# A convolution and token-mixing kernel: stretches of 64 rows in four quadrants of TensorE

## The chip, the core and the metric

The kernel runs on one core of a Trainium2 chip. The metric is the device time of one execution in microseconds (us). A profile of one execution is at hand; "span" is the time from its first to its last instruction. The engines are called by the profile's names: PE is TensorE's matmul, PEld its weight load, DVE is VectorE, ACT is ScalarE, POOL is GpSimd (it issues the loads of x here), SP issues the other transfers.

## What is computed

Eight batches of x, 4224 rows by 192 columns, go through a causal convolution along the rows: seven taps, one set of weights for each of 8 heads of 24 columns, with the weights put through a softmax. On its result y a token mixer follows:

```python
w = softmax(weight, axis=-1)                      # 8 heads x 7 taps
y[b, s, h, :] = sum_k w[h, k] * x_pad[b, s + k, h, :]   # 6 rows of zeros ahead
W_tok = scale * (y @ w_q) @ (y @ w_k).T           # 4224 x 4224 for each batch
out = relu(W_tok @ y) @ w_out
```

The kernel never makes the 4224 x 4224 matrix. It forms the Gram matrix y.T @ y (192 x 192) of a batch, multiplies it by w_k into mixing weights of 64 x 192, and applies these to y @ w_q. Matmuls are in bf16 with sums in f32.

## The kernel before

**Tiling of x and the convolution.** A batch is cut into 35 chunks of 122 rows (`CW`, `NCC`). For each chunk a window of 128 rows of x, six of them shared with the chunk before, lies across the 128 partitions: `XW[:, slot, chunk, :]`, cast from f32 to bf16 by the transfer itself. Five batches of x have a slot (`NX`). A matrix `BAND[:, h, :]` (128 x 128) holds the taps of head h along its diagonals. `gen_conv` multiplies it with the 24 columns of the head of all 18 or 17 chunks of a group at once, so with 432 or 408 moving columns (batch 0 has four smaller groups). It is done as one matmul over the whole array (line 356) or as two matmuls on the two column halves (lines 357 and 358); helper `halves` chooses by the mode of the operation. VectorE or ScalarE then copies the result to `Y` as bf16 (line 693).

**From y to the output.** `gen_transpose` turns the low 128 columns of each chunk (line 362 whole, lines 363 and 364 by column halves), eight chunks to a bank of the accumulation memory, and VectorE copies them to `YTL` (line 724). `gen_transpose_hi` turns the high 64 columns of two chunks side by side (line 754), copied to `YTH` (line 764). `gen_wq` projects both with w_q (lines 783 and 787) into `WQT`. `gen_gram` accumulates the Gram matrix, three matmuls a chunk (line 821). `gen_mix_weights` makes the mixing weights. `gen_mix` applies them (lines 914, 926 and 934), takes the ReLU into `RT` (lines 951 and 952), multiplies with w_out (lines 980 and 998), copies to `OUT` (line 1019) and stores.

**Shapes of the array.** An operation on TensorE has a mode: the whole array (128x128), two column halves (128x64) or two row halves (64x128). In the profile a matmul's shape stands as rows*columns: `128*64` or `122*64` is a column half, `64*128` a row half, `128*128` or `122*128` the whole.

**The order of the work.** All operations are generated in a simple order and numbered as they come. The string `PLAN`, written out by hand or by a program, then sets the order in which they are handed to the engines: `43S` is operation 43 on SP, `80P3` operation 80 on TensorE with bank 3, F in place of P means the whole array, A, D and G are ScalarE, VectorE and GpSimd. Each engine works through its operations in that order; waits between the engines come from the dependences (`Program.place`). Loads of a batch wait for the convolution of the batch that had the slot before.

**The start.** TensorE multiplies zeros (`run_up`, line 382, 512 columns each) while the taps are computed: four, then five of these, then two fills of the taps' bands (`spread`), then one more, and then the convolution of batch 0. The first load of x is the first thing that POOL issues, before it builds the identity matrix.

Of the kernel before, what the change touches and what calls it, by code (L numbers as in the profile page):

```python
# [13 lines left out]
PLAN = """  # L14
42G 0S 43S 1D 23A 2D 14G 9D 5D 6D 7D 4D 41G 45G 46G 47G 48G 62G 63G 64G 65G 16P3 10D 11D 12D 15D 20D 21D
17P2 19A 18P5 22D 24D 25D 26D 28A 27A 44A 49S 29D 31D 30D 32D 33D 34P4 37P1 40P7 38D 39D 3D 35A 78P0 36A
80P3 81D 82P1 83A 84P7 85D 79A 114P3 140P7 92P0 93A 66G 67G 115D 90F1 91A 88F6 89D 86F0 87A 98F4 99D 13D
94F6 95A 100F5 50S 101A 96F0 116F3 97A 117D 142P 141P 102F2 103D 108F5 109A 104F4 106F3 107D 8D 51S 118F0
119D 124P6 125D 105A 122F5 123D 120F4 121D 144P 126P2 127D 128P1 129D 143P 145P 146D 54A 52A 53A 130P6 131D
138P7 139A 132P3 159P1 160D 161A 56A 156F4 157A 158D 153F6 154A 155D 162F1 163A 164D 136P0 137D 134P5 135D  # L20
133A 55A 147F4 148A 181F7 182D 183F6 184D 207P4 174P0 175D 176D 168P2 59A 57A 58A 149P5 152A 151A 150A 165P6
209P 171P0 166A 167D 249P5 169D 170A 172A 173D 208P 235P6 252D 238A 61A 221P0 224A 185P1 186D 195P7 196D
191P5 192D 220P2 222A 60A 68G 189P6 190D 223D 287P0 187P7 211P 205P2 206D 188D 210P 193P5 194D 290P2 288A
289A 291D 292A 293P0 294A 295A 284P6 285D 286A 212P 199P5 200A 69G 299P2 300A 197P1 198A 213D 214P0 301D
234P6 215D 236D 237A 225P4 229P2 226P 227A 248P0 250A 251A 230P 231D 232D 263P6 266A 228D 233S 70G 71G 314P7
315D 203P4 204A 201P2 277P3 279A 72G 73G 74G 75G 76G 77G 110G 111G 112G 113G 177G 178G 179G 180G 308G 309G
239P0 243P5 276P4 278D 240P 241D 202A 242A 312F7 313D 244F 245D 246A 247S 216F4 218A 262P0 264D 217A 265A
219A 253P2 257P6 280P5 254P 255D 256A 258P 259A 281P 282D 283S 305P0 306A 352P4 296P2 297A 298A 302P5 303A
338P0 260D 261S 307D 418P1 419A 420A 355A 340P 311G 304D 320P3 321D 324P5 325D 351P6 353D 354A 316F1 317D
366F2 369A 424F3 425D 426A 430F6 431D 432A 310G 342P 322P2 326P1 327D 271P4 323D 267P6 318F3 319D 272F 273A  # L30
274D 268F 269D 270A 275S 427F1 428D 429A 380F3 383D 334P4 335A 336P5 337D 339P 421P6 422A 423D 415P1 416A
417D 330P4 331A 332P3 333A 365P6 367D 368A 360P1 356P4 361P 362D 363A 357P 407P6 409D 358D 359A 364S 328P3
329A 394P7 397A 374P1 370P5 375P 376A 377D 379P3 371P 372A 373D 378S 381A 441F7 433F1 434D 435A 436F5 437D
438A 442D 408P3 341P 343P 344D 447P6 448D 451P5 452D 439P2 440D 345P7 410A 382A 384P3 346A 393P0 395A 388P5
347F7 349A 348A 396D 350A 385F 386A 387D 389F 390A 391D 392S 445F0 446D 478P1 480A 481D 402P3 411P5 398P6
403P 404D 405A 412P 413A 414S 399F 548F0 549D 550D 400A 401A 406S 443F4 444D 493P5 560P2 561A 562A 496D
479P6 482A 453P0 449P7 542P1 543A 454D 465P4 450D 545P5 546A 547D 461P3 462A 459P1 460D 507P0 510A 468P
506P6 508D 509A 463P5 557P0 558A 559D 544D 455P3 456A 464A 469P 563P6 564A 565D 551P0 552A 553D 466P 457P5
458D 483P6 492P2 494A 495D 487P0 484F 485D 486A 568F5 569D 488F 489D 490A 491S 497P2 470P 535P7 537A 554F5
555D 556A 498F 499D 500A 566F7 567D 521F1 524A 501P5 520P2 522A 523A 534P0 536A 502P 503D 504D 505S 467P  # L40
576P1 577D 574F7 575D 675F2 676D 677D 471A 472F5 473A 538P4 515P0 511P6 570F5 571D 474F2 477A 476A 475A 539F
540D 541S 572F3 573D 516P 517A 518D 512P 513A 514A 519S 525P4 578P2 580P0 581D 526F 527A 528D 669F6 670A
648F3 651A 672F0 671A 678F4 590P6 591A 679A 579D 586P2 587A 680A 592P3 594P 582P7 583A 673D 674D 606P0 620P6
609D 529P1 605P4 607D 530P 531A 634P7 637D 532A 533S 608A 623D 595P 584P0 585A 588P2 597P 589A 614P4 633P6
635A 636D 610P0 615F 616A 617D 693F2 694D 611P 661P6 612A 613D 618S 619P4 621D 593P 662P7 622A 664A 596P
647P1 628P4 663A 624P6 649A 650A 598D 599F3 600D 629F 630A 631D 625F 626A 627D 632S 684F0 685A 686D 601F2
604A 603A 602A 695F4 696D 642P6 638P0 643F 644D 645A 690F2 691A 692D 681F4 682D 683A 639F 640D 641A 646S
687F6 688D 689A 656P2 652P4 665P1 657P 658D 659A 653P 666P 667D 668S 733P0 736A 747P7 750D 703P6 704D 705P3
706D 654A 655A 660S 707P2 708D 796P0 797A 798A 697P7 698D 802P5 803A 804D 805P3 761P0 764A 806D 799P1 800A
801A 699P5 700D 732P6 701P0 702D 807D 709P3 710D 734A 811P1 812D 813A 717P0 718D 715P6 716A 735A 822P5 823D  # L50
820P3 821D 713P1 714A 711P2 712A 737P6 746P4 748A 749D 741P0 738F 739A 740D 775F2 778A 742F 755P4 788P3
751P6 743A 744D 745S 756P 757A 758A 760P1 762A 763D 790D 752P 753A 719P0 721P 808P4 754A 759S 789P3 929P1
723P 809A 810D 817P6 818D 819D 938P4 939D 940A 791A 724P 722P 720P 725A 930D 931A 774P6 776D 777A 765P4
792P3 769P0 793P 794A 795S 766P 767A 768D 770P 726P2 771D 772A 773S 727A 814P6 815A 846P3 848P 728P5 730A
729A 731A 816D 828P7 829D 824P6 825D 834P2 926P0 835D 826P4 827D 923P5 924D 832P2 833D 830P7 831D 927A 928A
925A 932P0 933A 842P4 860P6 863D 847P 844P7 845D 874P5 877D 934A 843D 840P1 841A 836P0 837D 851P 783P6 779P1
859P4 861D 862A 784P 785A 786A 780P 781D 850P 888P0 891A 782D 787S 849P 852A 935P5 838P4 936A 937D 839A
853P2 854D 949P3 950D 868P0 873P6 864P4 875D 876A 902F2 905A 869F 870A 871D 865F 866A 867D 872S 947F3 948D
901P6 903A 915P2 917D 882P0 904A 878P4 883P 884A 885D 916P3 918A 879P 880D 881A 886S 887P6 889D 890A 855F2
858A 944F0 945D 946A 941F3 942A 943D 857A 856A 919P5 910P6 892P0 911P 912D 913A 896P3 920P 921A 922S 893P  # L60
897P 898D 951P2 952D 959P7 961P6 962D 957P5 958D 953P3 954D 960D 894A 895A 899A 900S 955P0 956D 973P4 987P1
990D 971P2 972A 1001P5 1004A 963P6 964A 967P7 968A 906P2 986P0 988D 989A 907P 1014P5 908D 909A 914S 1016A
1017D 978P 1015P7 1018A 976P 1000P0 1002D 1003A 991P2 995P5 992P 993D 994A 1029F7 1032A 996P 997A 998D 999S
1009P0 1005P2 1010P 1011A 1012A 1028P6 1006P 1007A 1008D 1013S 1042P5 1044D 1030A 1031D 977P 974P 975P 979D
1043P2 1045A 965P0 966D 1023P5 1019P2 980F4 981D 1024F 1025D 1026A 1020F 1021D 1022A 1027S 982F7 985A 983A
984A 1033P0 1046P6 1034P 1035D 1036A 1037P4 1047P 1048D 1049S 1050P2 1052A 1038P 1039A 1040D 1041S 969P7
1051P6 1054A 1081F0 1066F5 1069A 1053D 970D 1065P1 1067D 1068A 1055P3 1056P 1057D 1058A 1059S 1084A 1060P6
1070P1 1061P 1062D 1063A 1064S 1080P4 1082A 1083D 1071F 1072A 1073D 1074S 1096F0 1099A 1075P6 1095P3 1097D
1098A 1076P 1077D 1078A 1079S 1090P1 1091P 1092A 1093D 1094S 1110P0 1112D 1100P3 1085P6 1101P 1102D 1103A
1104S 1111P5 1086P 1087D 1113A 1114P4 1105P2 1115P 1116A 1117S 1106P 1088D 1089S 1107D 1108D 1109S  # L70
""".split()

COL2, ROW2, FULL = "128x64", "64x128", "128x128"


class Op:
# [4 lines left out]
    def __init__(self, engines, emit, ns, needs=(), after=(), banks=0, drains=None, vt=0.0, mode=COL2, tail=0.0, whole=False):  # L81
# [12 lines left out]
        self.mode = mode  # L94

        self.whole = whole
# [12 lines left out]

        self.size = 0  # L110
        Op.n += 1
        self.id = Op.n


class Planner:

    ENGINES = {"P": "PE", "F": "PE", "A": "ACT", "a": "ACT", "D": "DVE", "d": "DVE", "G": "POOL", "S": "SP"}
# [106 lines left out]
def bass_lightweight_conv__then__hypermixer_token_mlp_kernel(  # L224
# [427 lines left out]
    def gen_conv(b, gi):  # L652
# [6 lines left out]
        for hp in range(H // 2):  # L659
# [25 lines left out]
            def evac(e, op, t0, t1, hp=hp, mm=mm):  # L685
                o = mm.bank * 512
                if nb == 1:
                    t0, t1 = 0, 2
# [424 lines left out]
```

## Time and profile before

| what | value |
|---|---|
| three runs | 167.82, 168.00, 168.57 us; median 168.0 |
| span of the profiled execution | 167.4 us |
| TensorE busy | 155.4 us, 2843 matmuls |
| VectorE, ScalarE busy | 132.4 us, 118.5 us |
| copies of y (line 693) | ScalarE 33.8 us in 71, VectorE 31.6 us in 57 |
| copies of the transposed y (lines 724 and 764) | VectorE, 40 and 24 of them |
| queue of x loads | 35616 packets, 13.41 MB as written |
| queue of stores and other loads | 12528 packets, 26.71 MB |

The time of a run is taken outside the program, so it lies a little above the span of the profiled execution. A busy time of TensorE is not a measure of its work, since matmuls overlap and their ends are modelled; the steps from one start to the next are.

### The profile page before, as it was taken

The numbers are of one execution on the slowest core, as the hardware profiler recorded it, in microseconds if no ns is written. First come the engines' busy times: TensorE is split into PE (matmuls) and PEld (weight loads), VectorE is DVE, ScalarE is ACT, GpSimd is POOL, SyncE is SP. The second block draws the span as 40 slices with busy tenths as digits, with TensorE's granted clock in tenths as the row PEclk, the third lists the DMA queues.
The fourth block names the chain that finished last, engine by engine and source line by source line (L and its number), as shares of the span: only waits on it lengthen the run. The fifth ranks groups of instructions, "written<-read, shape, count | busy, mean of one in ns | idle before, by whom it ended". The sixth has DMA issues, their size and how long they took to land.

```text
span 167.4 us, 6574 instructions
## 1 busy us (share of the span) xinstructions
PE 155.4 (93%) x2843; PEld 117.7 (70%) x2851; DVE 132.4 (79%) x277; ACT 118.5 (71%) x288; POOL 30.2 (18%) x39
## 2 busy tenths in 40 slices
PE   7589999999999999999999999999999999999930
PEld 2277948887777677787776768779888767785620
DVE  5554889987979699888976789976798888878950
ACT  3426357879975978877597788985856895969920
POOL 7999553535400200000000000000000000000000
PEclk9957999999999999999999999999999999999997
DMA  1999999999999999999999999999330585487996
GB/s 41 205 190 185 205 191 193 192 194 191 265 326 272 269 267 317 290 289 192 285 292 289 254 284 315 319 230 367 125 112 4 221 341 215 193 306 279 377 366 235
DMA packets 48172, 40.52 MB, mean 242 GB/s; under 512 B 37136, under 2 KB 40976, under 8 KB 48144
## 3 DMA queue, kind: packets, MB, share of 16 engines
q0 software_dynamic: 35616, 13.41, 66.8%
q1 hardware_dynamic: 12528, 26.71, 44.4%
q8 instruction: 22, 0.36, 0.9%
q14 instruction: 6, 0.05, 0.1%
HBM read 27.56 MB, written 25.95 MB: 320 GB/s over the span
## 4 chain that ended last, share of the span: by engine, by line
PE 85%; ACT 5%; DMA 2%; DVE 2%; issue 2%; DVEq 0%
PE ps L821 15%; PE ps L980 12%; PE ps L998 9%; PE ps L357 7%; PE ps L356 6%; PE ps L783 5%; PE ps L914 5%; PE ps L362 5%; PE ps L754 5%; PE ps L787 4%; PE ps L363 4%; PE ps L934 3%; PE ps L358 3%; DMA wt_f<-in_weight_dram 2%; ACT rt L951 2%
## 5 line engine op out<-in xcount | busy, mean ns | idle before, releaser
L951 ACT ACTIVATE rt<-ps 128x512 bf16<-128x512 f32 (+1 forms) x70 | 37.7, 560 | 5.9 <-PE ps L914 3.7
L693 ACT CAST y<-ps 122x432 bf16<-122x432 f32 (+2 forms) x71 | 33.8, 519 | 11.2 <-PE ps L358 9.1
L1019 DVE COPY out_sb<-ps 128x384 f32<-128x384 f32 (+1 forms) x64 | 32.8, 540 | 6.1 <-PE ps L998 4.6
L1019 ACT COPY out_sb<-ps 128x384 f32<-128x384 f32 (+1 forms) x72 | 31.5, 479 | 8.8 <-PE ps L998 8.2
L693 DVE CAST y<-ps 122x408 bf16<-122x408 f32 (+2 forms) x57 | 31.6, 587 | 6.5 <-PE ps L358 3.1
L578 POOL DMA_DIRECT2D xw<-in_x_dram x34 | 29.8, 904 | 25.1 <-issue 16.9
L821 PEld LDWEIGHTS ps<-y 122*64 122x64 bf16 x840 | 29.4, 112 | 3.6 <-issue 0.9
L821 PE MATMUL ps<-y 122*64 122x192 bf16 (+2 forms) x840 | 31.9, 223 | 0.0
L952 DVE TENSOR_SCALAR rt<-ps 128x512 bf16<-128x512 f32 (+1 forms) x42 | 26.0, 628 | 6.3 <-PE ps L914 4.6
L724 DVE COPY ytl<-ps 128x976 bf16<-128x976 bf16 (+1 forms) x40 | 23.2, 588 | 4.0 <-PE ps L364 3.0
L998 PE MATMUL ps<-wol,rt 64*128 64x192 bf16 (+1 forms) x264 | 25.1, 248 | 0.7 <-PE ps L998 0.3
L980 PE MATMUL ps<-woh,rt 64*128 64x192 bf16 x264 | 22.9, 248 | 0.8 <-ACT rt L951 0.4
L357 PE MATMUL ps<-xw,band 128*64 128x432 bf16 (+2 forms) x82 | 19.6, 347 | 0.1
L358 PE MATMUL ps<-xw,band 128*64 128x432 bf16 (+2 forms) x82 | 19.6, 349 | 0.0
L998 PEld LDWEIGHTS ps<-wol,rt 64*128 64x128 bf16 (+1 forms) x264 | 15.9, 114 | 4.4 <-PE ps L980 1.0
L804 ACT CAST wqt<-ps 128x512 bf16<-128x512 f32 (+1 forms) x26 | 13.7, 547 | 6.6 <-PE ps L787 6.5
L980 PEld LDWEIGHTS ps<-woh,rt 64*128 64x128 bf16 x264 | 12.5, 113 | 7.9 <-issue 1.7
L980 PE MATMUL ps<-wol,rt 64*128 64x192 bf16 x175 | 15.4, 243 | 0.0
L783 PE MATMUL ps<-ytl,wql 128*64 128x512 bf16 (+1 forms) x72 | 14.7, 367 | 0.2
L787 PE MATMUL ps<-yth,wqh 128*64 128x512 bf16 (+1 forms) x72 | 14.9, 361 | 0.0
L914 PE MATMUL ps<-wqt,msb 64*128 64x512 bf16 (+1 forms) x72 | 13.8, 363 | 0.0
L356 PE MATMUL ps<-xw,band 128*128 128x408 bf16 (+3 forms) x62 | 12.9, 333 | 0.1
(118 smaller groups left out, 207.9 us busy)
## 6 DMA issues: line engine op xcount, KB each, us to landing
out_dram<-out_sb SPq DMA_DIRECT2D x28, 768.0 KB, 7.2
xw<-in_x_dram POOLq DMA_DIRECT2D x7, 816.0 KB, 36.5
xw<-in_x_dram POOLq DMA_DIRECT2D x7, 768.0 KB, 38.6
out_dram<-out_sb SPq DMA_DIRECT2D x8, 384.0 KB, 4.3
out_dram<-out_sb SPq DMA_DIRECT2D x8, 96.0 KB, 5.2
xw<-in_x_dram POOLq DMA_DIRECT2D x1, 432.0 KB, 7.8
xf<-in_x_dram SPq DMA_DIRECT2D x1, 384.0 KB, 4.7
xw<-in_x_dram POOLq DMA_DIRECT2D x1, 384.0 KB, 6.3
```

Source lines behind the costliest of these rows:

```text
L357: e.matmul(out[0:64], lhsT[:, 0:64], rhs, **k)
L358: return e.matmul(out[64:128], lhsT[:, 64:128], rhs, **k)
L578: lambda e, op, part=part: e.dma_start(*part),
L693: return e.copy(dst, src) if op.engine == "ACT" else e.tensor_copy(dst, src)
L724: lambda e, op: e.tensor_copy(YTL[:, b % NYT, t0:t1], bank(mm_l.bank).bitcast(BF16)[:, 0:cols]),
L783: last = e.matmul(ps[64 * i : 64 * i + DH, 0:n], WQL[:, :], YTL[:, b % NYT, starts[i] : starts[i] + n], start=True, stop=False)
L821: mm = e.matmul(bank(where.bank)[p : p + 64, o : o + z - r], Y[0:w, yb, c, r : r + 64], Y[0:w, yb, c, r:z], start=st, stop=end, skip_group ...
L951: return e.activation(dst, src(), AF.Relu)
L952: return e.tensor_scalar(dst, src(), 0.0, None, op0=ALU.max)
L980: last = e.matmul(bank(op.bank + a)[:, (i - q) * D : (i - q) * D + D], RT[p, slot, a if lo else 2, i:n:nt], WOL[p, :] if lo else WOH[p, :] ...
L998: last = e.matmul(bank(fh.bank + a)[:, (i - q) * D : (i - q) * D + D], RT[p, slot, a, i:n:nt], WOL[p, :], start=False, stop=True, skip_gro ...
L1019: return e.copy(dst, src) if op.engine == "ACT" else e.tensor_copy(dst, src)
```

## The change

Stretches have 58 rows instead of 122, from windows of 64 rows. There are 37 on the lower 64 partitions, for the first half of a batch, and 36 on the upper 64, for the second half. The first window of the batch begins with 16 rows of zeros. Four batches of x have a slot instead of five.

The convolution runs in 64x64 mode: two row halves (first and second half of the batch) by two column halves (even and odd stretches), so that each step of a head is four matmuls on the four quadrants, with 240 and then 216 columns. `Y` then holds two stretches in one column, 64 partitions each, so 37 columns (19 and 18) with 116 rows of the batch each.

```diff
-    CW = 128 - (KC - 1)
-    NCC = (S + CW - 1) // CW
+    CW = 64 - (KC - 1)
+    NCC = -(-S // (2 * CW))
...
-    NX, NY, NYT = 5, 3, 2
+    NX, NY, NYT = 4, 3, 2
...
-    run_2 = run_up(5, after=[turned])
+    run_2 = run_up(12, after=[turned])
...
-    run_3 = run_up(1, after=fills)
+    run_3 = run_up(3, after=[fill])
...
+                for i in range(hn):
+                    h = hn * hp + i
+                    for r in range(2):
+                        rows, n = slice(64 * r, 64 * r + 64), ns[r]
+                        for p in range(2):
+                            last = e.matmul(
+                                bank(op.bank + r)[64 * p : 64 * p + 64, i * n * GRP : (i + 1) * n * GRP],
+                                BAND[rows, h, :],
+                                XW[rows, slot, 2 * g[0] + p : 2 * (g[0] + n) : 2, GRP * h : GRP * h + GRP],
+                                start=True,
+                                stop=True,
+                            )
```

Each half of the batch has a bank of its own and its own copy to `Y`: 480, 480, 432 and 384 columns where before 432 and 408 stood. The loads of a group are one for each half of the batch, and the rows behind the zeros make a third in the first group.

The low transpositions run in 64x128 mode, the two stretches of a column of `Y` on the two row halves, into two banks; the high ones run in 64x64 mode, four at a time. The copies out of them take both banks at once and put the stretches back in order, in pieces of 58:

```diff
+    TG = [(0, 10), (10, NA)]
+
+    def blocks(e, op, src_bank, dst, n):
+        src = PS[:, src_bank * 512 : (src_bank + 2) * 512].bitcast(BF16).rearrange("p (i m) -> p i m", i=2)
+        src = src[:, :, 0 : n * CW].rearrange("p i (k t) -> p i k t", t=CW)
+        return e.tensor_copy(dst.rearrange("p (k i t) -> p i k t", i=2, t=CW), src)
...
         def tr_lo(e, op):
...
             for k in ks:
                 for i in range(2):
+                    rows = slice(64 * i, 64 * i + CW)
                     last = e.transpose(
+                        bank(op.bank + i).bitcast(BF16)[:, (k - k0) * CW : (k - k0 + 1) * CW],
+                        Y[rows, yb, r * NA + k, 0:LO],
+                        IDENT[rows, 64 * i : 64 * i + CW],
                     )
...
+                    for r in range(2):
+                        last = e.transpose(
+                            bank(op.bank + i).bitcast(BF16)[64 * r : 64 * r + HI, (k - k0) * CW : (k - k0 + 1) * CW],
+                            Y[rows, yb, r * NA + k if r == 0 or k < NBC else k, LO:D],
+                            IDENT[rows, 64 * i : 64 * i + CW],
+                        )
```

There are four copies of 1160, 1160, 1044 and 928 columns to `YTL` and two of 1160 and 1044 to `YTH` for a batch, instead of five and three. The Gram matrix is summed over 37 columns of `Y` instead of 35 chunks. The projection reads its last block of 128 rows in two spans. The taps' bands are 128 x 64 and filled in one operation.

`PLAN` is new throughout, since operations and numbers are others. Behind each TensorE entry stands its mode: F whole, C column halves, R row halves, Q quadrants. Its beginning and its end:

```diff
+PLAN = """1D 2D 9D 0S 5D 6D 16G 7D 4D 47G 43S 12D 18F6 44S 46G 13D 14D 17D 22D 23D 24D 40G 41G 11D 26D
...
+1044S 1059S 1064S 1074S 1079S 1087S""".split()
```

16 is the identity matrix, 40 to 42 are the loads of batch 0's first group, 46 and 47 those of its second. The new order has 1088 entries, 445 of them on TensorE, 245 on VectorE and 303 on ScalarE; the old one has 1118, with 470, 277 and 287.

More of the change, by code (lines that the diff above doesn't have):

```diff
@@ L20 @@
[L20 to L29, printed above, removed]
@@ L256, in groups_of, with columns, windows @@
     def groups_of(b):
-        cuts = [0, 9, 18, 27, NCC] if b == 0 else [0, 18, NCC]
-        return [list(range(c, z)) for c, z in zip(cuts, cuts[1:])]
+        cuts = [0, 5, 10, 15, NA] if b == 0 else [0, 10, NA]
+        return list(zip(cuts, cuts[1:]))
+    def columns(r, g):
+        return range(g[0], min(g[1], NA if r == 0 else NBC))
+    def windows(r, g):
+        return range(2 * g[0], min(2 * g[1], NCC if r == 0 else NB))
     es = contextlib.ExitStack()
@@ L487, in bass_lightweight_conv__then__hypermixer_token_mlp_kernel, with spread @@
     taps.needs.append(own)
+    def spread(e, op):
+        last = None
+        for half in range(2):
+            for q in range(4):
+                for p in (0, 64):
+                    last = e.matmul(
+                        bank(op.bank + half)[p : p + 64, 64 * q : 64 * q + 64].rearrange("p (i h) -> p i h", h=4),
+                        STEPT[0:112, 112 - 16 * q : 176 - 16 * q],
+                        TAPS[0:112, :, 4 * half : 4 * half + 4],
+                        start=q == 0,
+                        stop=q == 3,
+                        skip_group_check=True,
+                    )
+        return last
@@ L490, in bass_lightweight_conv__then__hypermixer_token_mlp_kernel @@
+    fill = add("PE", spread, 235, needs=[taps, stept], after=[run_2], drains=run_2, banks=2)
     bands = []
-    fills = []
     for half in range(2):
-        def spread(e, op, half=half):
-            last = None
-            for q in range(8):
-                last = halves(
-                    e,
-                    bank(op.bank)[:, 64 * q : 64 * q + 64].rearrange("p (i h) -> p i h", h=4),
-                    STEPT[0:112, 112 - 16 * q : 240 - 16 * q],
-                    TAPS[0:112, :, 4 * half : 4 * half + 4],
-                    start=q == 0,
-                    stop=q == 7,
-                    skip_group_check=True,
-                )
-            return last
-        fill = add(
-            "PE", spread, 215, needs=[taps, stept], after=[run_2, *fills], drains=None if fills else run_2, banks=1
-        )
-        fills.append(fill)
-        for pair in range(2):
-            def band(e, op, h0=4 * half + 2 * pair, k=2 * pair, fill=fill):
-                dst = BAND[:, h0 : h0 + 2, :]
-                src = bank(fill.bank).rearrange("p (j h) -> p h j", h=4)[:, k : k + 2, :]
-                return e.copy(dst, src) if op.engine == "ACT" else e.tensor_copy(dst, src)
-            bands.append(add("ACT" if half == 0 else "DVE", band, 320, drains=fill))
@@ L520, in bass_lightweight_conv__then__hypermixer_token_mlp_kernel, with band @@
-    run_3 = run_up(1, after=fills)
-    turns = [zero_r, one, zero_x, eps, zero_e, zero_x0[0], zero_s, zero_q, *zero_k, step, by_tap, other]
-    turns += [own, mx, sub, mine, sm, rc, own_sm, wn, taps, *bands[2:], zero_w, zero_m, zero_x0[1]]
+        def band(e, op, half=half):
+            dst = BAND[:, 4 * half : 4 * half + 4, 0:CW]
+            src = bank(fill.bank + half)[:, 0:256].rearrange("p (j h) -> p h j", h=4)[:, :, 0:CW]
+            return e.copy(dst, src) if op.engine == "ACT" else e.tensor_copy(dst, src)
@@ L524, in bass_lightweight_conv__then__hypermixer_token_mlp_kernel @@
+        bands.append(add("ACT" if half == 0 else "DVE", band, 330, drains=fill))
+        bands[half].part = half
+    run_3 = run_up(3, after=[fill])
+    turns = [zero_r, one, zero_x[0], eps, zero_e, zero_x0[0], zero_s, zero_q, *zero_k, step, by_tap, other]
+    turns += [own, zero_b, mx, sub, mine, sm, rc, own_sm, wn, taps, bands[1], zero_w, zero_m, zero_x0[1], zero_x[1]]
     for p, op in zip(turns, turns[1:]):
```

437 lines of the change are left out of this document (207 added, 230 removed).

## The prediction

> **What bounds the kernel now.** I read the page first (busy shares, the forty slices, the chain that ended last), then the windows stage by stage, the groups of instructions with shapes kept apart, and TensorE's timeline.
>
> ```profile
> PE 155.4 (93%) x2843; PEld 117.7 (70%) x2851; DVE 132.4 (79%) x277; ACT 118.5 (71%) x288; POOL 30.2 (18%) x39
> ...
> DMA  1999999999999999999999999999330585487996
> ...
> HBM read 27.56 MB, written 25.95 MB: 320 GB/s over the span
> ...
> PE 85%; ACT 5%; DMA 2%; DVE 2%; issue 2%; DVEq 0%
> ```
>
> TensorE carries 85% of the chain. Its last matmul ends at 161.0 us, 6.4 us before the end, so 167.4 - 155.4 - 6.4 = 5.6 us is all its idle time before that, and over half of it lies ahead of the first convolution at 8.17 us. The windows agree; after the length their columns are PE, PEld, DVE, ACT, POOL (busy, instructions), granted clock, DMA share, GB/s:
>
> ```profile
> 8.20:15.00 6.80, 6.13 (x66) 4.64 (x67) 3.57 (x8) 2.49 (x6) 6.80 (x9) 0.50 1.58 190
> ```
>
> ```profile
> 45.00:115.00 70.00, 69.47 (x1254) 53.30 (x1256) 58.90 (x116) 56.28 (x132) 1.71 (x2) 1.00 1.29 284
> ```
>
> From 45 to 115 us TensorE idles for 0.5 us, while VectorE and ScalarE are busy 84% and 80%. In the first line the clock is at half. The second thing to see is the DMA row: 0.9 or more up to some 120 us. Between 20 and 40 us only x moves, written as bf16 at some 190 GB/s, so read as f32 at twice that, 378 GB/s.
>
> So a change counts by what it does to TensorE's time, until the DMA or the copying engines take over. The timeline tells how that time is spent:
>
> ```profile
> 31.87 0.35 PE L357 MATMUL ps<-xw,band 128*64 128x432 bf16 x1
> 31.87 0.35 PE L358 MATMUL ps<-xw,band 128*64 128x432 bf16 x1
> 32.05 0.34 PE L357 MATMUL ps<-xw,band 128*64 128x432 bf16 x1
> ...
> 32.24 0.22 PE L363 MATMUL ps<-ident,y 122*64 122x122 bf16 x1
> ...
> 32.29 0.21 PE L363 MATMUL ps<-ident,y 122*64 122x122 bf16 x1
> ```
>
> ```profile
> 62.26 0.33 PE L980 MATMUL ps<-woh,rt 64*128 64x192 bf16 x4
> 62.52 0.23 PE L356 MATMUL ps<-gsb,wkl 128*128 128x128 bf16 x1
> ```
>
> The second column is a modelled duration; the steps from start to start count. Two column halves start together, and a pair of N columns takes about N/2.4 + 3 ns: 0.18 us for 432, 53 ns for 122. Row halves (L980) overlap too, 0.08 us a pair of 192. Where the tile shape changes (here 64*128 to 128*128) more is paid: 62.26 plus two pairs is 62.42, yet the next starts at 62.52. Over the 99 changes of shape in the trace the typical step is 92 to 99 ns longer than N/2.4. I take **96 ns a change**, 9.5 us for 99.
>
> **The change part by part**, per batch, then times 8.
>
> Convolution: now 8 heads x (183 + 173 ns) = 2.85 us. After, four quadrants of 240 and then of 216 columns: if all four overlap, starting 3 ns apart as halves do, 8 x (109 + 99) = 1.66 us, so **-9.5 us** in all. No row shows quadrants. Bounds: two pairs in turn, 8 x (2 x 103 + 2 x 93) = 3.14 us or +2.3 in all, and the full -9.5. I take the latter, since rows show each halving to overlap.
>
> Low transpositions: now 35 x 53 ns = 1.84 us. After, 37 pairs of row halves with 58 columns. The nearest row is the spreading of the taps, pairs of 64 columns that start 30 to 32 ns apart:
>
> ```profile
> 7.20 0.19 PE L357 MATMUL ps<-taps,stept 112*64 112x64 bf16 x1
> 7.20 0.20 PE L358 MATMUL ps<-taps,stept 112*64 112x64 bf16 x1
> 7.23 0.20 PE L357 MATMUL ps<-taps,stept 112*64 112x64 bf16 x1
> 7.23 0.20 PE L358 MATMUL ps<-taps,stept 112*64 112x64 bf16 x1
> ```
>
> Less six columns that is 28.5 ns: 37 x 28.5 = 1.05 us, **-6.3 us**. Bounds: two in turn (57 ns, +2.2 us), and this.
>
> High transpositions: now 18 x 53 = 0.95 us. After, 19 steps of four quadrants with 58 columns: 24 + 9 = 33 ns, 0.63 us, **-2.6 us**. Bounds: 33 ns, and two pairs in turn (57 ns, +1.0 us).
>
> Gram: L821 takes 88 ns a chunk; 37 chunks instead of 35, **+1.4 us**. Projection, mixing and output matmuls keep their columns. The spread halves (-0.25 us), but the first convolution waits for x there, so I count nothing.
>
> Changes of shape: the new order writes a mode behind each of its 445 TensorE entries (F, C, R, Q), and read in sequence it changes 195 times. 96 more at 96 ns: **+9.2 us**. Half of what the tiles save is given back here. Bounds: nothing where TensorE would have waited anyway, and all of it; with 0.5 us of waits in 70, I take all.
>
> Start: 6.8 us ran at half clock after TensorE had idled from 5.25 to 7.05 us. The longer run-up (12 and 3 instead of 5 and 1; 427 ns each at half clock, 213 at full) closes that gap. At most half of 6.8 is won, 3.4 us. Against it, the POOL queue now has the identity ahead of the first x load, and five x loads (some 0.8 MB as bf16, 4.3 us at 180 GB/s) ahead of the first convolution's last rows, which then land near 9.5 us instead of 8.12. I take **-1.5 us**, between 0 and -3.4.
>
> Copies: y rows grow from 6720 to 7104 columns a batch; at 0.54 to 1.04 ns a column (432 against 408 in the groups) that is 1.7 to 3.2 us over both engines. The transposed copies are 48 instead of 64, 1160 columns at most; by the rows 656 ns for 976 and 316 ns for 320 (0.52 ns a column, 150 fixed) they save some 1.8 us. So the 251 us of the two engines stay near 252, 16 entries go from VectorE to ScalarE, and at 159 us both are near 79%: cover remains. But each transposition now holds two banks instead of one, and x comes later (below). **+1.0 us** of new waits, between 0 and +6.
>
> DMA: 64-row windows read 8 x 4656 rows instead of 8 x 4428, 28.97 MB with the weights. Hidden, see the second rival. Four slots of x instead of five: loads of batch 4 wait for batch 0's convolution, done near 20 us, while the queue is still busy with batch 3 up to 43 us; nothing.
>
> Sum: 167.4 - 9.5 - 6.3 - 2.6 + 1.4 + 9.2 - 1.5 + 1.0 = 159.1 us of span. The three runs lie 0.4 to 1.2 us above the profiled span, their median 168.0 by 0.6: **159.7 us**.
>
> **Rivals.**
>
> *The quadrants do not overlap all four (the change does not do what it says).* Place: convolution and high transpositions. Price: 8 x 1.47 + 8 x 19 x 24 ns = 15.4 us, so 175, slower. It decides from 28 ns a step of four on: 8.3 us over 144 + 152 steps. For it: no quadrant in the trace. Against: both halvings overlap. 6%.
>
> *x becomes late.* All traffic, 54.9 MB at 378 GB/s, takes 145 us, from 4.5 us on. Until x is in, outputs (3.24 MB per 18 us, from 40 us on) share the rate: 29.0 + 0.179 (T - 40) = 0.378 (T - 4.5) gives T = 118; the same sum gives 108 for before, where the last x landed at 114, so some 123. Batch 7's last convolution began at 128.75 us, 14.6 after its x; 7 us sooner it has no slack. Some 4 us: 164. 12%.
>
> *An issue floor.* The spread shows 15.6 ns a matmul (32 in 0.50 us) and nothing shows less. As a floor it makes a high step 62 ns and a low one 31: +5.1 us, 165. 6%. A floor of 25 ns each would make them 100 and 50: +16.6 us, 176, slower; 3%, as the lines above start four in 60 ns. The Trainium skill, "TensorE: Matmul & The Clock Gate", section "Wait — 56ns, not 53.3ns?", states such a floor of about 25 ns from start to start however few the columns; this trace disagrees for column halves, at 15.6 ns.
>
> *VectorE loses its double rate* on the transposed copies, now cut into pieces of 58: 6496 columns a batch at 0.52 ns more, +27 us. VectorE, at some 121 after the moves, would need 148; at the 90% that it reaches from 20 to 45 us that is 165, and some 5 us at the ends: 170. For it, no such pattern in the trace; against, 58 stays a run of neighbours. 4%.
>
> *Better:* full clock from the start, no new waits: 154. 9%.
>
> **How the numbers follow.** The forecast, 155 to 163.5, holds 60%. About 0.5% is what a measurement of this kernel can tell from no change. Faster by more: 60 + 12 + 6 + 9, less 2 for tails, 85%; same 3%; slower 12%. The range 153 to 166 takes in the late x, the mild floor and half of the better case, some 80%.
>
> **What would show it.** Steps of four near 109 and 33 ns, row pairs near 28 ns; about 195 changes of shape at 96 ns; clock at full from 8 us; TensorE's idle time between 8 us and its last matmul below some 4 us; last x near 123 us with its convolution right behind. Steps of four over 137 ns, or VectorE copies of 1160 columns over 1 us, would prove me wrong.

## The result, and the profile after

| | time | span of the profiled execution |
|---|---|---|
| before | 168.28 us, median of 4 runs (167.82 to 169.90) | 167.4 us |
| after | 198.72 us, median of 4 runs (197.48 to 200.96) | 196.1 us |

The ratio is 1.176 (95% interval 1.168 to 1.184). The change makes the kernel slower by 30 us; the prediction was 159.7 us. The ratio leaves out runs over 1.5% above the fastest of the same kernel, here the one of 200.96 us. The lines of the page after that answer to those of before:

```profile
PE 162.1 (83%) x3789; PEld 111.1 (57%) x3789; DVE 126.0 (64%) x245; ACT 127.9 (65%) x304; POOL 35.2 (18%) x49
...
PEclk9975698799699999789988999999999978999997
DMA  3999999999999999999999444624083926084796
...
q8 instruction: 30, 0.49, 1.0%
...
HBM read 28.96 MB, written 25.95 MB: 280 GB/s over the span
...
PE 73%; issue 10%; DMA 6%; DVE 3%; ACT 2%; SPq 2%; DVEq 0%
```

TensorE no longer fills the span, no other engine took its place (VectorE and ScalarE fell from 79% and 71% to 64% and 65%), and the DMA row leaves 9 after slice 22. The chain of what ended last has 10% of "issue": time in which the engine waited for nothing that the profile knows. The clock row dips five more times. The windows of the two stages that the prediction showed, with the same columns:

```profile
8.20:15.00 6.80, 4.16 (x124) 3.11 (x124) 3.98 (x9) 1.84 (x4) 6.80 (x9) 0.83 1.55 186
45.00:115.00 70.00, 57.24 (x1341) 40.22 (x1337) 42.34 (x78) 45.64 (x107) 10.04 (x13) 0.93 1.24 237
```

From 45 to 115 us TensorE now idles for 12.8 us instead of 0.5. Yet the tiles do what the prediction took them to do. TensorE's timeline at full clock, in a stretch without stops:

```profile
118.63 0.40 PE L651 MATMUL ps<-xw,band 64*64 64x240 bf16 x8
118.86 0.51 PE L739 MATMUL ps<-ident,y 58*64 58x58 bf16 x40
119.25 0.30 PE L651 MATMUL ps<-xw,band 64*64 64x240 bf16 x4
```

The second row holds ten steps of four: 0.51 us less the 0.19 us that one such matmul is given is 32 ns a step. So the time was not lost in the tiles. The list of waits says where, by engine, line, what released it, sum, times and longest:

```profile
PEld ps L814 <- issue: 9.4, 16, 2.3
PE ps L814 <- issue: 6.2, 5, 2.1
...
PEld ps L651 <- issue: 5.6, 11, 2.0
ACT wkt L596 <- DMA whi<-in_moe_w_k_dram: 4.9, 1, 4.9
...
PEld ps L779 <- issue: 4.4, 8, 2.5
```

The line differs from stop to stop (gram, convolution, projection, output), and the releaser is always "issue". Four of the stops in the timeline:

```profile
26.52 0.14 PEld L814 LDWEIGHTS ps<-y 128*64 128x64 bf16 x4 [1.73 <-issue]
...
32.78 0.38 PE L779 MATMUL ps<-ytl,wql 128*64 128x512 bf16 x1 [2.16 <-issue]
...
48.77 0.43 PE L814 MATMUL ps<-y 128*64 128x192 bf16 x8 [2.10 <-issue]
...
101.05 0.36 PE L973 MATMUL ps<-wol,rt 64*128 64x192 bf16 x4 [2.60 <-issue]
```

**What the stops have in common.** I numbered TensorE's instructions (matmuls, weight loads and the 118 waits of its sequencer, 7696 in all) in order of time and noted the number of the first one after each stop:

| resumes at, us | instruction no. | (no. - 194) / 256 | lost, us |
|---|---|---|---|
| 26.52 | 706 | 2.00 | 1.76 |
| 32.78 | 961 | 3.00 | 2.33 |
| 42.41 | 1219 | 4.00 | 0.93 |
| 48.77 | 1474 | 5.00 | 2.27 |
| 55.08 | 1729 | 6.00 | 0.38 |
| 61.31 | 1986 | 7.00 | 0.95 |
| 68.04 | 2242 | 8.00 | 1.20 |
| 74.30 | 2498 | 9.00 | 1.83 |
| 80.52 | 2754 | 10.00 | 2.58 |
| 94.65 | 3266 | 12.00 | 0.91 |
| 101.05 | 3523 | 13.00 | 2.76 |
| 107.46 | 3778 | 14.00 | 1.01 |
| 158.18 | 6337 | 24.00 | 1.99 |

Each stands at the start of a block of 256 instructions; together they cost 20.9 us. The queue "instruction" in the page moves packets of 16,384 bytes, 30 of them after and 22 before, which is about one for each 256 of the 7696 and 5800 TensorE instructions. In the trace's transfer records, TensorE resumes 1.3 to 1.5 us after the end of such a packet at all 13 stops. While x is loaded, the packet starts 2.8 to 7.1 us after TensorE has begun a block, in nine of fourteen blocks 3.8 to 4.0, and takes 0.95 us: 3.9 + 0.95 + 1.4 = about 6.3 us for a block, and eight of the ten blocks that lie between two stops took 6.2 to 6.4 us. Between 114 and 153 us, when x is in, the packet starts 0.2 to 1.1 us after a block is begun, and blocks are used up in 3.9 to 6.1 us without a stop. The last stop, at 158 us, came while outputs alone moved; its packet started 3.0 us after the block was begun.

**The theory of the supply**, then: while x is loaded, TensorE gets no more than about 256 instructions in 6.3 us, some 41 per us. The kernel before was already at that limit: its packets end 1.4 to 5.6 us before the next block begins, and at 32.8, 39.0 and 73.9 us only 1.4 us before, no more than the 1.3 to 1.5 us that a stopped TensorE takes to go on. The change cut the work into smaller matmuls, a third more instructions, and ran into it. The windows from 20 to 47 us, before and then after:

```profile
20.00:47.00 27.00, 26.98 (x538) 20.50 (x532) 23.62 (x49) 20.80 (x55) 11.18 (x13) 1.00 1.55 209
```

```profile
20.00:47.00 27.00, 21.96 (x541) 14.90 (x533) 15.77 (x30) 17.24 (x43) 11.21 (x14) 0.88 1.56 206
```

In this stage TensorE started 538 + 532 = 1070 matmuls and weight loads before and 541 + 533 = 1074 after: the same number, but each now carries less work. The rivals: the small tiles or the new order themselves, and the start.

### The profile page after: what moved, and what is told of

Same layout as the page of the kernel before. It is cut to its first block, busy times and chain, and to the rows that moved or that the text cites. A ratio compares the mean times of both kernels' runs of the same rounds, so it can differ in the third digit from the quotient of the medians.

```text
span 196.1 us, 8451 instructions
## 1 busy us (share of the span) xinstructions
PE 162.1 (83%) x3789; PEld 111.1 (57%) x3789; DVE 126.0 (64%) x245; ACT 127.9 (65%) x304; POOL 35.2 (18%) x49
## 4 chain that ended last, share of the span: by engine, by line
PE 73%; issue 10%; DMA 6%; DVE 3%; ACT 2%; SPq 2%; DVEq 0%
PE ps L814 15%; PE ps L973 12%; PE ps L651 10%; PE ps L779 9%; PE ps L991 9%; PE ps L711 5%; PE ps L907 5%; PE ps L927 4%; DMA whi<-in_moe_w_k_dram 3%; DMA xf<-in_x_dram 3%; PE ps L739 3%; PE ps L919 1%; SPq L587 1%; ACT y L675 1%; DVE ytl L697 1%
## 5 line engine op out<-in xcount | busy, mean ns | idle before, releaser
L675 ACT CAST y<-ps 128x480 bf16<-128x480 f32 (+2 forms) x77 | 38.4, 539 | 16.7 <-PE ps L651 16.2
L944 ACT ACTIVATE rt<-ps 128x512 bf16<-128x512 f32 (+2 forms) x69 | 36.1, 558 | 12.1 <-PE ps L907 6.0
L814 PE MATMUL ps<-y 128*64 128x128 bf16 (+2 forms) x888 | 35.7, 228 | 6.2 <-issue 6.2
L675 DVE CAST y<-ps 128x480 bf16<-128x480 f32 (+3 forms) x51 | 29.9, 607 | 13.5 <-PE ps L651 13.3
L814 PEld LDWEIGHTS ps<-y 128*64 128x64 bf16 x888 | 31.0, 115 | 12.6 <-issue 9.4
L1012 DVE COPY out_sb<-ps 128x384 f32<-128x384 f32 (+1 forms) x54 | 28.5, 546 | 12.8 <-PE ps L991 12.3
L697 DVE COPY ytl<-ps 128x1160 bf16<-128x1160 bf16 (+2 forms) x32 | 22.5, 714 | 17.1 <-PE ps L711 15.8
L945 DVE TENSOR_SCALAR rt<-ps 128x512 bf16<-128x512 f32 (+2 forms) x43 | 26.3, 629 | 7.3 <-PE ps L907 3.9
L651 PE MATMUL ps<-xw,band 64*64 64x240 bf16 (+5 forms) x576 | 24.2, 271 | 4.4 <-issue 2.6
L711 PE MATMUL ps<-ident,y 58*128 58x58 bf16 x592 | 14.5, 194 | 5.7 <-ACT y L675 4.7
L711 PEld LDWEIGHTS ps<-ident,y 58*128 58x128 bf16 x592 | 12.2, 98 | 8.4 <-ACT y L675 3.8
L779 PE MATMUL ps<-yth,wqh 128*64 128x512 bf16 (+1 forms) x80 | 15.2, 364 | 0.0
```

The source lines that it names most:

```text
L651: last = e.matmul(bank(op.bank + r)[64 * p : 64 * p + 64, i * n * GRP : (i + 1) * n * GRP], BAND[rows, h, :], XW[rows, slot, 2 * g[0] + p ...
L675: return e.copy(dst, src) if op.engine == "ACT" else e.tensor_copy(dst, src)
L697: return e.tensor_copy(dst.rearrange("p (k i t) -> p i k t", i=2, t=CW), src)
L711: last = e.transpose(bank(op.bank + i).bitcast(BF16)[:, (k - k0) * CW : (k - k0 + 1) * CW], Y[rows, yb, r * NA + k, 0:LO], IDENT[rows, 64 ...
L779: last = e.matmul(ps[64 * i : 64 * i + DH, c : c + w], WQL[:, :] if lo else WQH[:, r, :], src, start=lo and (nh == 2 or k == 0), stop=not ...
L814: mm = e.matmul(bank(where.bank)[p : p + 64, o : o + z - d], Y[:, yb, c, d : d + 64], Y[:, yb, c, d:z], start=st, stop=end, skip_group_che ...
```

## The experiments

**1. More instructions in the kernel before, same columns (e8_dense).** Nothing of the change is in it.

```diff
-                for p, r, z, o, st in ((0, 0, D, 0, begin), (64, 64, D, 64, begin), (64, LO, D, 0, False)):
+                for p, r, a, z, o, st in (
+                    (0, 0, 0, 96, 0, begin),
+                    (64, 64, 64, 128, 64, begin),
+                    (0, 0, 96, D, 96, False),
+                    (64, 64, 128, D, 128, False),
+                    (64, LO, LO, D, 0, False),
+                ):
```

> The kernel before, with the same gram columns cut into more matmuls: each chunk has five instead of three, the two column halves still in turn, so the step of a chunk should stay near 88 ns. TensorE has about 6810 instructions instead of 5694 and no more columns. Theory of the supply: blocks of 256 hold 6 us of work or less instead of 7.3, so TensorE stops at block ends while x is loaded, 5 to 12 us in all, with spells at half clock after the long ones: 174 to 184 us. Rival (more instructions cost nothing while each matmul is hidden): the step stays at 88 ns and the time within 1.5 us of the kernel before, 167 to 170 us.

Measured: 185.43 us (184.69 to 186.28), ratio 1.097 (1.091 to 1.103). The span grew by 16.3 us; stops at eight block ends (instructions 705, 961, 1218, 1473, 1985, 2499, 3009 and 5313) make 13.7 us of it, and the step of a chunk, 95 ns instead of 87, 2.2 us (280 chunks). One stop and the stage:

```profile
33.75 0.32 PE L827 MATMUL ps<-y 122*64 122x64 bf16 x8 [2.02 <-issue]
```

```profile
20.00:47.00 27.00, 20.51 (x491) 15.16 (x487) 18.13 (x37) 14.31 (x37) 10.66 (x12) 1.00 1.60 192
```

So instructions alone, without quadrants, new order or new loads, make the same stops. They and the time lie a little over what was expected. The clock stayed at full after them, which the expectation had otherwise (the section on why the prediction was wrong comes back to this).

**2. A first form of the same (e1_dense)**, each of the three gram matmuls cut into two halves one behind the other.

```diff
+                    half = (z - r) // 2
+                    for part in range(2):
...
+                            bank(where.bank)[p : p + 64, o + part * half : o + part * half + half],
```

> The kernel before, its order untouched, with every Gram matmul cut in two by columns: the same columns in all, 840 matmuls and 840 weight loads more (7374 TensorE instructions, about as many as the changed kernel's 7578). Supply theory (TensorE's instructions come in blocks of 256, one 16 KB packet each, and while x is loading a block takes about 6.2 us from the start of the block before): up to 112 us the old kernel used a block in 7.3 us, now it would in 5.7, so TensorE must stop at block ends, with nothing that it waits for in the profile, and the clock falls after the stops: 180 to 190 us. Rival (the new order's own waits, or tiles that do not overlap, made the changed kernel slow; the number of instructions is no matter): 840 more starts at 3 ns, 171 us at most.

Measured: 191.84 and 194.85 us. Stops at seven block ends, 11.3 us by the same count. But the step of a chunk rose from 87 to 126 ns, 280 x 39 ns = 10.9 us, since neighbouring matmuls now lie in the same column half and no longer overlap. This run mixes two causes; experiment 1 was made to part them.

**3. Less x (e2_half_x).** The kernel after with the loads of batches 4 to 7 cut to one window each, so that half of the output comes from the data of other batches. Instructions and order stay.

```diff
+            if b >= NX:
+                w1 = w0 + 1
```

> The changed kernel, with the loads of x for batches 4 to 7 cut to one window each (the rest of a slot keeps the batch that was there before, so half of the output is of other data). Supply theory: the DMA is free of x after some 45 us, blocks of instructions come in time, and the stops of 0.4 to 2.8 us at block ends between 46 and 108 us (some 14 us) go, with four spells of half clock (1.7 us each): 176 to 180 us; the stops before 45 us stay. Rival that the order itself makes TensorE wait: 195 to 199. Rival that x comes late: also faster, but then the stops that go are ones that a load of x had ended, and in the profile of the changed kernel none was.

Measured: 182.79 us (182.01 to 183.58), ratio 1.081 (1.072 to 1.091), 16 us faster than the kernel after. The windows with x still loading and with x in:

```profile
20.00:47.00 27.00, 19.53 (x488) 14.70 (x480) 15.47 (x28) 15.60 (x39) 8.40 (x14) 0.89 1.54 203
47.00:105.00 58.00, 55.74 (x1476) 40.71 (x1478) 44.23 (x81) 48.00 (x115) 5.17 (x10) 1.00 0.52 185
```

After the last x TensorE starts 2954 instructions in 58 us, 51 per us; the kernel after starts 1088 + 1092 = 2180 there. Up to 47.4 us the stops stay (8.2 us); later ones make 4.7 us, so the time is 2 us or more above the range expected. With the order and the tiles as they were, most stops went with x: it is mainly the transfers of x that make blocks late. The later stops came while outputs moved, so transfers of outputs delay packets too, but less.

**4. Fewer instructions, more work (e5_wide).** The kernel after with transpositions over whole columns of y.

```diff
-            for k in ks:
-                for i in range(2):
-                    rows = slice(64 * i, 64 * i + CW)
...
-                        Y[rows, yb, r * NA + k, 0:LO],
-                        IDENT[rows, 64 * i : 64 * i + CW],
+            for k in range(ne):
+                c = r * NA + min(k0 + k, ks[-1])
...
+                    Y[:, yb, c, 0:LO],
+                    IDENT[:, :],
```

> The kernel after, with the transpositions over whole columns: a low one takes all 128 rows of a column of y in one matmul of 128 moving columns instead of two row halves of 58, a high one two column halves of 128 instead of four quadrants of 58. Everything else stays. TensorE has about 6380 instructions (matmuls and weight loads) instead of 7578, and about 11 us MORE of matmul time at the steps measured (27 ns a pair and 32 ns a four become some 53 ns each). Theory of the supply (TensorE stops at the end of blocks of 256 of its instructions while x is loaded): the stops at block ends, 20.9 us in the kernel after, go down to under 8 us, most of the 27 us at half clock goes with them, and the time falls to 178 to 190 us although TensorE has more to do. Rival (the small tiles or the new order are at fault): the time rises by the added work, to some 205 to 212 us.

Measured: 186.62 us (186.42 to 187.53), ratio 1.105 (1.099 to 1.111): 12 us faster than the kernel after, although the steps rose from 27 to 56 ns (low) and from 32 to 56 ns (high), some 12 us over eight batches. Stops at block ends: 3.5 us instead of 20.9; half clock outside start and end: none.

```profile
20.00:47.00 27.00, 25.52 (x533) 18.70 (x531) 17.92 (x34) 18.74 (x49) 11.20 (x14) 0.95 1.58 204
```

Again 1064 instructions in this stage, now with TensorE busy for 25.5 us. This run decides against the rival that the whole loss is small tiles or order: it keeps the order and the quadrants of the convolution. The parts (17.4 us of stops, 7.6 of clock and 2.4 at the start won, 12.2 lost) sum to -15.2 us, while the span fell by 11.6; 3.6 us I could not place.

**5. Smaller loads of x (e3_pieces).** Each load in pieces of four windows.

```diff
-                lambda e, op, part=part: e.dma_start(*part),
+                lambda e, op, cut=cut: [(e.dma_start(*p), 16) for p in cut],
```

> The changed kernel with each load of x issued in pieces of four windows (256 rows, 16 for each of 16 engines) instead of up to twenty; the same rows. In the changed kernel the packet of instructions starts about 3.8 us after the block before was entered while x loads, and 2.5 us or less after it later. If it queues behind a whole piece of x on its DMA engine, shorter pieces let it through earlier, blocks take about 5.3 us and the stops shrink to half: 180 to 188 us. If it only shares the rate with x, nothing changes: 196 to 200 us. GpSimd issues about 0.5 us for each piece, 150 pieces, well inside its idle time; if that is wrong, x itself comes later and it gets slower.

Measured: 194.52 us (193.26 to 196.62), ratio 1.148 (1.140 to 1.157). This lies between the two forecasts. In the profiled run (196.62 us, the slowest of the four) packets start 2.9 us after a block is begun, at the median of the blocks from 18 to 50 us, instead of 3.9; from 50 to 105 us it is 4.0 us in both kernels. A gain of some 4 us; ten stops of about 1 us or more stay.

**6. The start mended (e4_start).** In `PLAN`, the first load of x and then the identity ahead of the other loads on POOL; the ten weight casts (55A to 64A) behind the first batch's y.

```diff
-1D 2D 9D 0S 5D 6D 16G 7D 4D 47G ... 59A 85A 110D 111R2 62A ...
+40G 1D 2D 16G 9D 41G 42G 46G 47G 0S ... 55A 56A 57A 58A 59A 60A 61A 62A 63A 64A 121C3 ...
```

> The changed kernel with its start put right: the first group's loads of x lead POOL's queue (the first of them ahead of the identity matrix, as before), and the ten casts of weights on ScalarE, which the new order has among the first copies of y, come after batch 0's gram instead. It takes away the stop of 3.9 us at 14.6 us, where ScalarE waited 4.9 us for w_k's load with copies of y behind it, and lets the first convolution start at about 9 us instead of 10.9. If the clock then stays full from 12.6 to 22.8 us, 5 us more: 188 to 192 us. If the blocks of instructions set the pace anyway, the early gain is lost by 45 us: 196 to 199 us.

Measured: 195.30 us (194.18 to 196.55), ratio 1.155 (1.148 to 1.163). The stop of 3.9 us at 14.6 us is gone, but the block end at 21.0 us now stops TensorE for 3.7 us. Of the 6.6 us that the start lost (below), some 3 us are won; the rest of what the start gives, the next block takes.

**7. Both (e6_both).**

> The kernel after with both mends that were run alone: the loads of x in pieces of four windows, and the identity ahead with the ten weight casts later. Alone they gave ratios of 1.148 and 1.155 instead of 1.176. Theory of the supply: pieces shorten the wait of an instruction packet behind loads of x by 0.7 us a block, and the start gives 3.9 us that the next block end then mostly takes back; together 186 to 192 us, the stops at block ends while x is loaded still over 10 us. Rival (the start alone is the cause of what is lost): under 175 us.

Measured: 198.28 us (197.41 to 199.14), ratio 1.172 (1.166 to 1.179). The two gains do not add; they cancel. POOL issues 166 instructions instead of 49 and is busy for 97.9 us, and its issuing of loads is now 10% of the chain of what ended last: x itself is late in the first 33 us. The expectation missed this.

**8. Loads of x spread out (e9_paced).** A table names for each later load a TensorE entry to wait for, 17 to 19 us ahead of use.

```diff
+            if op.number in PACE:
+                op.needs.append(self.ops[PACE[op.number]])
```

> The kernel after with the loads of x spread out: from the second half of batch 1 on, each load waits for a TensorE entry that ran 17 to 19 us before the load's first use in the trace of the kernel after, instead of starting as soon as a slot is free (loads landed up to 60 us ahead of use). Instructions, tiles and order of TensorE stay. If the stops come from instruction packets that queue behind the loads of x, the stops at block ends after 22 us (18.5 us in the kernel after) fall under 8 us, most of the 17 us at half clock between 33 and 163 us goes, and the time is 174 to 186 us. Rival (a block has a fixed turnaround of some 6 us whatever else moves): the stops stay, 194 to 201 us. A second rival: x becomes late, seen as waits of the convolution on x, over 200 us.

Measured: 206.89 us (206.01 to 208.04), ratio 1.227 (1.221 to 1.233). Both the second rival and a miss of mine. The loads of batch 1 came too late:

```profile
33.41 0.41 PE L672 MATMUL ps<-xw,band 64*64 64x240 bf16 x4 [9.65 <-DMA xw<-in_x_dram]
```

And the stops did not go: six from 48 to 100 us make 11.1 us, and they now go on after 110 us too (1.5, 2.1, 2.3 and 1.8 us), because transfers do:

```profile
DMA  4990992299249999999999989992799968083796
```

The wait is not fixed: of the nine blocks begun between 50 and 100 us, three had their packet 0.6 to 1.3 us after the block was begun, two of these while hardly any x moved, and the six others 2.2 to 4.8 us after it. But over the run x and the outputs keep the DMA engines about as busy, and spreading x only spreads the stops.

**9 and 10. Spread loads with other mends (e10_mend, e11_pace_start).** The former also has whole-column transpositions and the mended start, the latter small tiles and the mended start.

> The kernel after with three mends: whole-column transpositions (about 1200 TensorE instructions fewer, some 11 us more of matmul time), the identity ahead and the weight casts later, and the loads of x spread out. The whole-column version alone took 186.6 us with 3.5 us of stops at block ends, 10 us at half clock and the gaps of the start left. Supply theory: 172 to 180 us, stops under 2 us. Rival (start and stops are not what is left): 184 us or more.

> The kernel after with its small tiles kept, the loads of x spread out, the identity ahead and the weight casts later. Supply theory: the stops in the first 25 us, where batch 0 and 1 of x must load at full rate, stay (some 4 to 6 us with a spell at half clock), the later ones fall under 8 us: 168 to 182 us. If the small tiles pay once the supply holds, this run beats the one with whole columns. Rival (fixed turnaround): 192 us or more.

Measured: 202.48 us (200.53 to 205.16), ratio 1.197 (1.189 to 1.204), and 205.21 us (204.88 to 207.22), ratio 1.220 (1.212 to 1.228). Both miss, for the same reason: of the chain of what ended last, 26% in the first and 16% in the second are transfers of x. They say nothing about the supply beyond experiment 8.

**11. Whole columns and the mended start (e12_wide_start).**

> The kernel after with whole-column transpositions, the identity ahead and the weight casts later; the loads of x as in the kernel after. The whole-column version alone took 186.6 us, with a stop of 2.0 us at 14.6 us and 10.2 us at half clock behind it. Where the later start was mended in the kernel with small tiles, the next block end took 3.7 us of it back. Theory: with fewer instructions a block holds more work, so the gain of the start is kept for the larger part: 180 to 184 us. Rival (the first blocks of instructions set the pace of the first 25 us whatever is mended there): 185 to 188 us.

Measured: 187.67 us (186.41 to 188.93), ratio 1.104 (1.097 to 1.111): not faster than experiment 4. The rival holds. The spread of the taps now waits for VectorE, which is busy with the first x,

```profile
9.46 0.32 PE L510 MATMUL ps<-taps,stept 112*64 112x64 bf16 x8 [3.07 <-DVE taps L494]
```

and the block end at 23.1 us stops TensorE for 2.1 us. Two trials at the start (6 and 11) did not win back most of what the start lost.

**12. The longer run-up alone, in the kernel before (e7_runup).**

```diff
-    run_2 = run_up(5, after=[turned])
+    run_2 = run_up(12, after=[turned])
...
-    run_3 = run_up(1, after=fills)
+    run_3 = run_up(3, after=fills)
```

> The kernel before with the run-ups of the change alone (12 and 3 instead of 5 and 1). The prediction took 1.5 us off for the start, between 0 and 3.4. If TensorE then reaches full clock ahead of the first convolution: 8.2 to 15.0 us runs at full clock and the time falls by 1.5 to 3.4 us, 164.6 to 166.5. Rival: the first blocks of instructions, or x itself, set the pace there: no change within 0.5%, or up to 1 us slower since the run-up itself delays the spread of the taps.

Measured: 167.99 us, median of 12 runs (167.63 to 169.34), against 168.88 (17 runs of before); ratio 0.995 (0.992 to 0.998). The clock part of the step is right, by the window from 8.2 to 15 us:

```profile
8.20:15.00 6.80, 5.79 (x115) 4.47 (x114) 4.26 (x9) 3.77 (x8) 6.80 (x9) 1.00 1.57 189
```

But 0.9 us comes of it, not 3.4: TensorE, now ahead, stops for 0.47 us at instruction 962, 3 x 256 + 194, where the kernel before did not. This is the only version here that beats both kernels, by half a per cent.

## Why the prediction was wrong

**The step that failed is "+1.0 us of new waits, between 0 and +6"**, with the sentence under it that VectorE and ScalarE keep cover at 79%. I looked for waits on banks, copies and x, the things that a dependence names. None of them ended TensorE's time. What ended it was the supply of TensorE's own instructions, which no rival held: 20.9 us of stops at block ends. It was to be seen before: "q8 instruction: 22" stood in the page, packets ended as little as 1.4 us ahead of need, and the change adds a third more instructions. Only the trace after shows that 1.4 us is no slack at all.

**The clock.** The prediction had half clock end at the start. After, TensorE ran at half clock from 12.7 to 22.9 us and in five spells of 3.41 us, each beginning 0.4 to 1.5 us after a stop of 2.0 us or more; 27.3 us in all. Less 3.9 us of standing still in the first, half of that is 11.7 us, where the sum had left 1.9: +9.8 us.

Why did stops of the same length leave the clock alone in experiment 1? In each trace all changes of the clock lie on one grid of 3.413 us, so the stop has to be measured inside the intervals of that grid. The traces of the 14 versions hold 657 whole intervals at full clock. In 38 of them TensorE had no matmul running for 1.74 us or more (by the modelled ends), and half clock followed all 38; in 610 it was 1.56 us or less, and it followed none; of the nine between, it followed four. So it took about half an interval of idle time. In the kernel after the five intervals ahead of a spell held 1.80 to 2.60 us; in experiment 1, from 15 us to the end of its stops, none held more than 1.71 us, as some stops were cut by the edge of an interval. That the idle share is the cause is read from this order alone; no run varied it by itself.

**The start, -1.5 us.** The first convolution came at 10.87 us instead of 8.17, late x as feared, but later than the 9.5 that I took: +2.7. Then a stop that I had not seen at all:

```profile
17.70 0.30 ACT L596 CAST wkt<-wlo 64x128 bf16<-64x128 f32 x1 [4.89 <-DMA whi<-in_moe_w_k_dram]
17.91 0.55 ACT L675 CAST y<-ps 128x480 bf16<-128x480 f32 x1
```

ScalarE stood for 4.9 us in a cast that waited for a weight, with a copy of y queued behind it, and TensorE's transposition waited for that copy: 3.9 us. The new order was read for modes, not for what stands behind a waiting entry. Together +6.6.

**Sum**: 159.1 + 20.9 + 9.8 + 6.6 = 196.4 us against a span of 196.1. The agreement is closer than the parts deserve: stops and half clock touch each other, and the convolution's steps (next table) were longer than predicted, some 2 us over eight batches by my estimate (64 steps at 18 ns and 64 at 14 ns more), which this sum leaves out.

**What held, and one that was off.** Medians of steps in the trace after, at full clock, against the prediction:

| | predicted | measured |
|---|---|---|
| convolution, four quadrants of 240 columns | 109 ns | 126 ns (102 to 127) |
| convolution, 216 columns in two quadrants, 192 in two | 99 ns | 113 ns |
| low transpositions, row pair | 28.5 ns | 27 ns |
| high transpositions, step of four | 33 ns | 32 ns |
| gram, a chunk | 88 ns | 87 ns |
| changes of shape | 195 at 96 ns | 195 at 96 ns |
| VectorE, 1160 columns | 150 + 0.52 x 1160 = 753 ns | 759 ns |

So the rivals that the quadrants do not overlap, that an issue floor holds, and that VectorE loses its double rate all fell, and x was not late in the end (the last load was issued at 89.8 us, its first use came at 155 us or later). The Trainium skill's floor of about 25 ns a matmul ("TensorE: Matmul & The Clock Gate", "Wait — 56ns, not 53.3ns?"), which was a rival at 176 us, is contradicted by 8 ns a matmul in quadrants. Ironically the overlap makes the failure worse: the cheaper a matmul, the faster a block of 256 is used up.

The Trainium skill names the mechanism ("Runtime: NRT & Kernel Launch", "Instruction fetch mechanics"): instructions come in blocks of 16 KiB, 256 of them, and it adds that the cost of crossing into the next is mostly hidden. Here that agrees with the trace after 110 us, but for the stop at 158 us, and not while x moves: from 26 to 108 us, 12 crossings cost 0.4 to 2.8 us each.

**What stays open.** That transfers of x delay the instruction packets is shown (experiment 3, and the kernel after with x and without); where in the queues they wait is not, nor why one packet, after 32.8 us, started only 7.1 us after the block was begun. Smaller loads shortened the wait by 0.9 us up to 50 us and not at all later, so the length of a load is a minor part of it. Why the convolution's steps came out at 102 ns in some places and at 127 in others was not looked into. How much of the loss the new order has of its own beyond the start was not tried.

## What to carry to other kernels

Count instructions per microsecond as well as columns: cutting a matmul into smaller ones that overlap is only worth its time while the blocks of instructions arrive, and under a saturated DMA they arrived here at no more than some 41 TensorE instructions per us, a rate that the kernel before had already reached at three of its block ends. When waits read "issue" on lines that differ from stop to stop, number the engine's instructions and look for a period, and compare the ends of the instruction packets with the block ends; the smallest slack in the kernel before, less the 1.3 to 1.5 us that TensorE takes to go on, tells what a denser stream may cost. And in a new order, look at every entry that waits for a transfer for what is queued behind it on its engine.

## What the hardware showed that I had not expected

- TensorE's instructions arrive in packets of 16,384 bytes for 256 instructions; beside the loads of x a packet starts 3.9 us after a block is begun, and 1.0 us after it when only outputs move (medians; 2.8 to 7.1 and 0.2 to 3.0 us).
- TensorE started nearly the same number of matmuls and weight loads from 20 to 47 us in kernels of very different work: 1070 (before), 1074 (after), 1064 (whole columns); in experiment 1 it was 978.
- Spells at half clock last 3.41 us or a multiple (10.24 us). The Trainium skill's window of 3413 ns ("TensorE: Matmul & The Clock Gate", "What's actually happening") agrees with these lengths. The Trainium skill asks there for at least one idle window before the clock falls; here it fell after stops of 2.0 to 2.8 us, and in the 14 traces whenever 1.74 us or more of an interval of the grid were idle.
- The order of matmuls decides whether halves overlap: the same chunk of the Gram matrix took 126 ns with neighbours in one column half (experiment 2) and 95 ns with the halves in turn, in five matmuls (experiment 1).
